# A transformer block on one core: seven products instead of eight in the down projection, and weight remainders on GpSimd

## The chip, the cores and the metric

The kernel runs on one core of one Trainium2 chip. TensorE multiplies matrices out of SBUF into PSUM (eight banks); VectorE, ScalarE and GpSimd work element by element, GpSimd on SBUF alone; SyncE only issues DMA transfers here. Each engine works off its own queue in order and waits on semaphores of the others. The time is microseconds (us) of the device for one execution.

## The reference

One pre-norm transformer block in float32, 2048 tokens of width 576: attention with 32 heads, then a gated feed-forward layer (GEGLU) with an inner width of 4608.

```python
h  = x + attention(layernorm(x), wqkv) @ wo
y  = layernorm(h)                             # 2048 x 576
g  = y @ w_gate                               # 576 x 4608
u  = y @ w_up                                 # 576 x 4608
h2 = h + (gelu(g) * u) @ w_down               # 4608 x 576
```

The change concerns the last three lines only, the feed-forward layer.

## The kernel before

**Two halves per number.** Every float32 operand of a matmul is scaled by a power of two and split into two float16 halves, `high = round(x)` and `low = x - high`. A product is then high·high + high·low + low·high, so three matmuls. Producing the two halves is work for ScalarE (the rounding, called `high` in the code) and VectorE or GpSimd (the remainder, called `low`).

**Tiling.** The inner width is cut into 18 chunks of 256 columns (`FC`); two chunks make a super chunk (`sc`, 0 to 8). The tokens are cut into two parts `p` of 1024, each of two blocks of 512 (`TB`).

**A unit** (`unit(c, p)`, line 1051) computes gate and up of one chunk for 1024 tokens, both by Strassen's scheme: seven products for gate and seven for up, alternating, each of 7 matmuls with 512 columns (`product`, line 1057). They go to six PSUM banks, g[0..2] and u[0..2]. Between products the other engines fetch the sums out of PSUM (`nc.scalar.copy`, `nc.vector.tensor_add`), apply `gelu` (ScalarE, L1070) and `gate` (VectorE, L1073), and split the result into float16 halves (`high`, ScalarE, L1076; `low`, GpSimd, L1079), the four pieces of `hts`. After each product the generator yields.

**A down stage** (`down(p, ...)`, line 1142) multiplies the pieces of two chunks with the super chunk's 512 rows of `w_down`: for each of 8 row blocks of 128 tokens and each half of the 576 columns one group of 12 matmuls with 288 columns, then one VectorE addition into the result `nat` (L1155).

**Weights.** `split_matrix` (line 927) prepares one chunk of `w_gate` or `w_up`: GpSimd forms the four sums that Strassen's scheme needs in place (L936), VectorE finds the largest magnitude (L129), a TensorE transpose spreads it (L138), VectorE turns it into a scale, ScalarE rounds three cuts of the seven pieces with that scale (L952) and VectorE subtracts (L966, L968). After the first cut's remainder the next matrix is loaded into the same place (`then`, L922 and L924). `split_down` (line 1021) does the like for `w_down`.

**Order.** Program order is kept on all engines (`manual_schedule`). The loop at line 1289 runs per super chunk: unit(c, 1), unit(c+1, 1), down(1), unit(c+2, 0), unit(c+3, 0), down(0), so the second half already works on the next super chunk. The preparation of weights is a second generator, `side`, and `beside` (line 1265) takes one step of it after each yield of a unit or a down stage, from yield number `head` on. Whatever such a step issues stands in each engine's queue right behind what the unit issued for the product just before.

Of the kernel before, what the change touches and what calls it, by code (L numbers as in the profile page):

```python
# [13 lines left out]
I32 = mybir.dt.int32  # L14
# [17 lines left out]
def tile_block(  # L32
# [61 lines left out]
    def view(region, off, shape, dtype=None):  # L94

        dtype = dtype or region.dtype
        v = region if dtype == region.dtype else region.bitcast(dtype)
        size = 4 if dtype == F32 else 2
        n = math.prod(shape)
        assert off % size == 0  # L100
        v = v[:, off // size : off // size + n]
        if len(shape) == 2:
            v = v.rearrange("p (a b) -> p a b", b=shape[1])
        elif len(shape) == 3:
            v = v.rearrange("p (a b c) -> p a b c", b=shape[1], c=shape[2])
        return v
# [61 lines left out]
    def pow2(e, a, b, name, pool=small):  # L168

        t = small.tile(list(e.shape), I32, tag=f"pi_{name}", name=f"pi_{name}")  # L170
        nc.vector.tensor_scalar(t, e, a, b, op0=ALU.mult, op1=ALU.add)
        r = pool.tile(list(e.shape), F32, tag=f"p_{name}", name=f"p_{name}")
        nc.vector.tensor_scalar(r.bitcast(I32), t, 23, None, op0=ALU.logical_shift_left)
        return r
# [127 lines left out]
    def run(it):  # L302
        for _ in it:
            pass
# [472 lines left out]

    VP = view(V, 0, (2 * PIECES, TB), F16)

    def piece(p, k):  # L780

        if k < 18:
            o = (2 * p + k // 9) * TB
            return XT[:, k % 9, o : o + TB]
        return VP[:, p * PIECES + k - 18]

    T4s = view(W, 23296, (HALF,), F32)

# [117 lines left out]
    dh = view(W, 6 * 2 * S, (4, D), F16)  # L906
    dl = view(W, 6 * 2 * S + 2 * 4 * D, (4, D), F16)
    hts = [[view(WK, 2 * 4 * TB * (2 * i + k), (4, TB), F16) for k in range(2)] for i in range(2)]
    ee = const.tile([P, 2, 2], I32, name="ee")

    def blank_rows():
# [15 lines left out]
    def split_matrix(c, m, hi_on=None, then=None, at=0, space=2, held=False):  # L927

        wh, wl = slots[c % 2][m]
        sums = [(nc.gpsimd.tensor_add, S1, A21, A22), (nc.gpsimd.tensor_sub, S2, S1, A11),  # L930
                (nc.gpsimd.tensor_sub, S3, A11, A21), (nc.gpsimd.tensor_sub, S4, A12, S2)]

        def add():
            if sums:
                op, d, a, b = sums.pop(0)
                op(W8[:, d], W8[:, a], W8[:, b])  # L936
# [15 lines left out]
        by = hi_on or (lambda dst, src, k: nc.scalar.activation(dst, src, AF.Copy, scale=k))  # L952
        cuts = ((4, 7), (0, 2), (2, 4))

        def high(k):
            if k < len(cuts):
                a, b = cuts[k]
                by(wh[:, a:b], W8[:, a:b], s)

        if held:  # L960
            yield "ready"
        high(0)
        yield
        for k, (a, b) in enumerate(cuts):
            high(k + 1)
            nc.vector.scalar_tensor_tensor(wl[:, a:b], W8[:, a:b, :2], s, wh[:, a:b, :2],  # L966
                                           op0=ALU.mult, op1=ALU.subtract)
            nc.vector.scalar_tensor_tensor(wh[r, a:b, 2], W8[r, a:b, 2], s[r], wh[r, a:b, 2],  # L968
                                           op0=ALU.mult, op1=ALU.subtract)
            if k == at and then is not None:  # L970
                then()
            yield
        if m == 0:
            scales[c % 2] = (pow2(e, 1, -20, f"gsc{c % 2}"), pow2(e, -1, 228, f"hsc{c % 2}"))

    scales = [None, None]

# [43 lines left out]
    def split_down(sc, at=(A, W8O)):  # L1021
# [22 lines left out]
        if at[0] is A:  # L1044
            blank_rows()

    banks = []
    tmps = []
    tmp_ring = ring(tmps)

    def unit(c, p):

        gsc, hsc = scales[c % 2]
        hh, hl = hts[c % 2]
        g, u = ([b[:, :TB] for b in banks[3 * i : 3 * i + 3]] for i in range(2))

        def product(m, bank, a, b, start):
            wh, wl = slots[c % 2][m]
            ks = [piece(p, 5 * b + k) for k in range(5)]
            mm = []  # L1060
            for k in range(2):
                mm += [(wh[:, a, k], ks[k]), (wh[:, a, k], ks[3 + k]), (wl[:, a, k], ks[k])]
            mm += [(wh[:, a, 2], ks[2])]
            for i, (w, x_) in enumerate(mm):
                nc.tensor.matmul(bank, w, x_, start=start and i == 0,  # L1065
                                 stop=i == len(mm) - 1,
                                 skip_group_check=not start)
# [10 lines left out]
        def low(i, j, v):  # L1078
            nc.gpsimd.tensor_sub(hl[:, 2 * i + j], v, hh[:, 2 * i + j])  # L1079

        xg, xu = next(tmp_ring), next(tmp_ring)
        product(0, g[0], A11, B11, True)
        nc.scalar.copy(xg, g[0])  # L1083
# [58 lines left out]
    def down(p, dsc, last):  # L1142
        for j in range(2):
            for i in range(TPB):
# [13 lines left out]
                if last:  # L1158
                    nc.sync.dma_start(ov[:, t], nat[:, t])


    def other_products():
        for b in range(1, NB):
# [125 lines left out]
    for sc in range(NCH // 2):  # L1289
        c = 2 * sc  # L1290
        last = sc == NCH // 2 - 1
        dsc = dscs[-1]
        if not last:
            g2, g3 = (split_matrix(c + 2, 0, None, lambda c=c: load_matrix(w_up, c + 2), held=True),
                      split_matrix(c + 3, 0, None, lambda c=c: load_matrix(w_up, c + 3)))
            u2, u3 = (split_matrix(c + 2, 1, None, lambda c=c: load_matrix(w_gate, c + 3)),
                      split_matrix(c + 3, 1, None, lambda sc=sc: load_down(sc + 1), 2))
            dn = split_down(sc + 1)
            side = chain(until_ready(g2))
        beside(unit(c, 1), side, head=0 if sc else 7)  # L1300
        run(side)
        if not last:
            side = chain(g2, pause(2), u2, pause(2), g3, pause(2), u3, pause(4), dn)
        beside(islice(u := unit(c + 1, 1), 13), side)
        run(u)
        beside(down(1, dsc, last), side, head=2)
        if last:
            break
        run(u2)
# [33 lines left out]
```

## Time and profile before

| what | value |
| --- | --- |
| runs | 2669.16, 2670.18, 2671.85 us, median 2670.18 |
| the profiled execution | 2668.08 us |
| its span, first to last instruction | 2666.3 us |
| TensorE matmuls busy over the span | 2589.7 us (97%) |
| VectorE, ScalarE, GpSimd busy | 2013.1, 1619.2, 777.3 us (76%, 61%, 29%) |
| granted TensorE clock, mean | 0.996 |

In the rows of the profile, PE is TensorE, PEld its weight loads, DVE is VectorE, ACT is ScalarE, POOL is GpSimd, SP is SyncE. A row of the timeline gives the start in the span, the duration, engine, source line, operation, output<-input, shape, count, and in brackets how long the engine sat idle before it and for whom. The feed-forward layer fills the span from about 1450 us on; the loop over super chunks repeats there every 132 us.

### The profile page before, as it was taken

To read this page: it belongs to the slowest core of one execution; us is meant where nothing else is said; L and a number is where in the kernel's file an instruction comes from. 1 tells how busy PE (TensorE), PEld (TensorE's weight loads), DVE (VectorE), ACT (ScalarE), POOL (GpSimd) and SP (SyncE) were. 2 spreads that over 40 slices of the span, in tenths; PEclk is the share of its full clock that TensorE was granted. 3 is DMA by queue.
4 is the path that set the end of the run, shared out by engine and by line. 5 is a ranking of instruction groups with operands and counts; after the bars stand their busy time and mean duration, and the time that the engine had idled before them with its cause. 6 is when DMAs were issued, how large, how long until landed. Compare 5 with 4: busy or idle time off the path is not lost.

```text
span 2666.3 us, 44517 instructions
## 1 busy us (share of the span) xinstructions
PE 2589.7 (97%) x16665; PEld 1118.6 (42%) x16665; DVE 2013.1 (76%) x3872; ACT 1619.2 (61%) x2128; POOL 777.3 (29%) x1040
## 2 busy tenths in 40 slices
PE   6999999999999999999999899999999999999999
PEld 2542222222222222222243555555555555555555
DVE  6367999999999999999967866566666666666653
ACT  5215999999999999999956433333333333333332
POOL 2200352132223232221666532222222222222221
PEclk9999999999999999999999999999999999999999
DMA  8411101010101010110116321010101010101010
GB/s 222 94 40 51 54 26 30 19 42 15 42 14 45 17 42 19 30 25 20 36 47 125 74 51 40 23 40 23 40 22 40 24 39 25 38 27 36 29 59 36
DMA packets 171466, 114.70 MB, mean 43 GB/s; under 512 B 90872, under 2 KB 149772, under 8 KB 171250
## 3 DMA queue, kind: packets, MB, share of 16 engines
q1 hardware_dynamic: 163566, 99.06, 13.9%
q0 software_dynamic: 7552, 12.79, 1.8%
q8 instruction: 130, 2.13, 0.3%
q14 instruction: 86, 0.70, 0.1%
q10 hardware_dynamic: 132, 0.01, 0.0%
HBM read 76.51 MB, written 15.01 MB: 34 GB/s over the span
## 4 chain that ended last, share of the span: by engine, by line
PE 67%; ACT 15%; issue 7%; DVE 4%; POOL 2%; DMA 2%; SPq 0%; ACTq 0%; DVEq 0%; POOLq 0%
PE more L1065 14%; PE bank L1065 13%; ACT WK L644 10%; PE bank L300 10%; PE bank L648 9%; PE more L300 8%; PE bank L589 7%; PE pair L300 4%; ACT nat L595 4%; PE pair L642 2%; DVE mx L601 1%; DMA nat<-rc 1%; ACT nat L662 0%; POOL A L996 0%; DMA V<-V 0%
## 5 line engine op out<-in xcount | busy, mean ns | idle before, releaser
L644 ACT ACTIVATE WK<-pair 128x1024 f32<-128x1024 f32 x1024 | 1000.0, 1041 | 84.8 <-PE pair L642 84.1
L601 DVE TENSOR_REDUCE mx<-bank 128x1 f32<-128x512 f32 x1552 | 975.7, 683 | 42.8 <-PE bank L589 32.4
L648 PE MATMUL bank<-WK,V 128*32 128x512 f32 x4096 | 547.7, 606 | 0.2 <-ACT nat L662 0.2
L300 PEld LDWEIGHTS <-WK 128*128 128x128 f16 x3456 | 338.0, 98 | 90.9 <-ACT WK L1076 1.7
L1065 PEld LDWEIGHTS <-W 128*128 128x128 f16 x2394 | 234.3, 98 | 282.9 <-issue 5.7
L589 PE MATMUL bank<-W 54*128 54x512 f16 x896 | 258.2, 379 | 14.0 <-DVE mx L601 1.8
L589 PE MATMUL bank<-A 54*128 54x512 f16 x904 | 255.0, 380 | 16.8 <-DVE mx L601 5.3
L671 POOL TENSOR_TENSOR rp<-rc,minus_one 128x16 f32<-128x16 f32 x28 | 81.9, 2926 | 537.1 <-DMA rc<-nat 537.1
L300 PE MATMUL more<-W,WK 128*128 128x288 f16 x1728 | 235.6, 286 | 2.2 <-ACT WK L1076 1.4
L300 PE MATMUL bank<-W,WK 128*128 128x288 f16 x1728 | 235.2, 286 | 0.0
L1065 PE MATMUL bank<-X,W 128*128 128x512 f16 x792 | 223.8, 379 | 0.0
L642 PE MATMUL pair<-A 56*128 56x512 f16 x1024 | 212.9, 381 | 2.3 <-ACT WK L644 1.4
L642 PE MATMUL pair<-W 56*128 56x512 f16 x1024 | 210.3, 380 | 4.3 <-ACT WK L644 3.2
L1065 PE MATMUL bank<-V,W 128*128 128x512 f16 x720 | 202.4, 379 | 0.4 <-ACT tmp L1115 0.3
L936 POOL TENSOR_TENSOR A<-A 128x384 f32<-128x384 f32 x136 | 137.0, 1028 | 202.6 <-DMA A<-in_B_w_up_dram 118.7
L589 PEld LDWEIGHTS <-W 54*128 54x128 f16 x1024 | 75.1, 93 | 283.6 <-issue 266.6
L599 DVE CUSTOM_DVE_ANT_0 nat<-bank,nat 128x512 f32<-128x512 f32 x248 | 171.4, 691 | 27.1 <-PE pair L642 4.4
L589 PEld LDWEIGHTS <-A 54*128 54x128 f16 x1024 | 72.3, 93 | 267.9 <-issue 250.8
L1079 POOL TENSOR_TENSOR WK<-tmp,WK 128x512 f16<-128x512 f32 x73 | 87.9, 1203 | 305.9 <-ACT WK L1076 305.6
L1083 ACT COPY tmp<-more 128x512 f32<-128x512 f32 x36 | 21.0, 583 | 236.8 <-PE more L1065 198.2
L595 ACT ACTIVATE nat<-bank 128x512 f32<-128x512 f32 x248 | 151.4, 611 | 11.5 <-PE bank L589 11.5
L648 PEld LDWEIGHTS bank<-WK,V 128*32 128x32 f32 x4096 | 81.1, 108 | 179.0 <-issue 164.2
(304 smaller groups left out, 3259.9 us busy)
## 6 DMA issues: line engine op xcount, KB each, us to landing
A<-in_B_w_down_dram SPq DMA_DIRECT2D x8, 1152.0 KB
nat<-rc SPq DMA_DIRECT2D x32, 256.0 KB
A<-in_B_w_gate_dram SPq DMA_DIRECT2D x64, 128.0 KB
A<-in_B_w_up_dram SPq DMA_DIRECT2D x64, 128.0 KB
qk_hi<-tmp SPq DMA_DIRECT2D x36, 128.0 KB
qk_lo<-tmp SPq DMA_DIRECT2D x36, 128.0 KB
out_dram<-nat SPq DMA_DIRECT2D x16, 288.0 KB
X<-nat SPq DMA_DIRECT2D x100, 36.0 KB
```

The source lines that it names most:

```text
L300: nc.tensor.matmul(dst, a, b, start=(i == 0), stop=(i == len(pairs) - 1))
L589: nc.tensor.matmul(pm[:, :TB], Q[r, q0 : q0 + P], keys, start=True, stop=True)
L595: nc.scalar.activation(row, pm[:, :TB], AF.Relu)
L599: nc.vector.tensor_tensor_reduce(row, pm[:, :TB], row, 1.0, LOWEST, ALU.add, ALU.max, dst)
L601: nc.vector.tensor_reduce(dst, pm[:, :TB], axis=AX.X, op=ALU.max)
L642: nc.tensor.matmul(pS[:, j, :TB], K[r, kt * P : (kt + 1) * P], Q[r, qc * TB : (qc + 1) * TB], start=True, stop=True)
L644: nc.scalar.activation(pes[(2 * kt + pr) % NPE], pS[:, :, :TB], AF.Exp, scale=ex_reg)
L648: nc.tensor.matmul(acc[32 * hh : 32 * hh + 32, :TB], Vg[n // NB][:, kt * G4 + hh * VC : kt * G4 + hh * VC + 32], pes[(2 * kt + hh // 2) % ...
L671: nc.gpsimd.tensor_tensor(rc, den, minus_one.to_broadcast([P, R]), op=ALU.pow)
L936: op(W8[:, d], W8[:, a], W8[:, b])
L1065: nc.tensor.matmul(bank, w, x_, start=start and i == 0, stop=i == len(mm) - 1, skip_group_check=not start)
L1079: nc.gpsimd.tensor_sub(hl[:, 2 * i + j], v, hh[:, 2 * i + j])
```

## The change

**Down by Strassen's scheme.** From super chunk 1 on the down stage is `down7`: seven products of 6 matmuls instead of eight blocks of 6, for each of four row blocks. It needs seven pieces of the gated activations instead of four (`unit7` forms H1 to H4 as sums and differences) and seven pieces of `w_down` (`split_down7`, sums on GpSimd). The unit's last products change places: A22 comes last, S4 before it. The PSUM banks change roles after each down stage.

**Remainders of gate and up weights.** From chunk 2 on ScalarE scales the float32 pieces in place and then rounds them, and GpSimd subtracts; the next load follows GpSimd's subtraction.

**Room.** The longer activation pieces lie where part of the layer's input pieces of tokens p=1 lay. The 15 input pieces that come last are stored to DRAM once for each p, and fetched in three parts, each after the product that used the old ones.

```diff
-    V = const.tile([P, 9936], F32, name="V")
+    V = const.tile([P, 10224], F32, name="V")
...
+    def keep_pieces(p):
+        nc.scalar.dma_start(xs[p], VP[:, p * PIECES + 2 : (p + 1) * PIECES])
+    def fetch_pieces(p, o):
+        nc.sync.dma_start(VP[:, 2 + 5 * o : 7 + 5 * o], xs[p][:, 5 * o : 5 * o + 5])
...
         def high(k):
             if k < len(cuts):
                 a, b = cuts[k]
-                by(wh[:, a:b], W8[:, a:b], s)
+                if c < 2:
+                    by(wh[:, a:b], W8[:, a:b], s)
+                else:
+                    nc.scalar.activation(W8[:, a:b], W8[:, a:b], AF.Copy, scale=s)
+                    nc.scalar.copy(wh[:, a:b], W8[:, a:b])
+        def low(a, b):
...
+            else:
+                nc.gpsimd.tensor_sub(wl[:, a:b], W8[:, a:b, :2], wh[:, a:b, :2])
+                nc.gpsimd.tensor_sub(wh[r, a:b, 2], W8[r, a:b, 2], wh[r, a:b, 2])
...
+    def split_down7(sc):
...
+        sums(0)
+        yield
+        high(0)
+        yield
+        low(0)
+        high(1)
+        sums(1)
+        yield
+        low(1)
+        high(2)
+        yield
+        low(2)
+        high(3)
+        yield
+        low(3)
+        yield
+        blank_rows()
...
+    def unit7(product, gelu, gate, g, u, hh, hl, used):
...
+        product(0, g[2], S4, B22, False)
+        nc.vector.tensor_add(ag, g[2], ag)
+        high(H22, bg)
+        gelu(ag, ag)
+        yield
+        product(1, u[2], S4, B22, False)
+        low(H22, bg)
+        nc.vector.tensor_add(au, u[2], au)
+        gate(ag, au)
+        nc.vector.tensor_add(xu, ag, bg)
+        yield
+        ga = next(tmp_ring)
+        product(0, g[0], A22, T4, False)
+        high(H1, xu)
+        gelu(ga, g[0])
+        low(H1, xu)
+        nc.vector.tensor_sub(bu, xu, xg)
+        high(H2, bu)
+        low(H2, bu)
+        yield
+        product(1, u[0], A22, T4, False)
+        used(2)
+        nc.vector.tensor_sub(au, xg, ag)
+        gate(ga, u[0])
+        high(H12, ga)
+        low(H12, ga)
+        high(H3, au)
+        low(H3, au)
+        nc.vector.tensor_sub(bg, ga, bu)
+        high(H4, bg)
+        low(H4, bg)
+        yield
...
+    def down7(p, dsc, last):
+        b0, b1, b2 = ((banks[i], banks[i + 3]) for i in (1, 0, 2))
+        def product(i, bank, a, b, start):
...
+            for k in range(2):
+                hh, hl = (v[:, a, tsl] for v in hts7[k])
+                mm += [(hh, dh7[:, k, b]), (hh, dl7[k][:, b]), (hl, dh7[:, k, b])]
...
+        for i0 in (0, 2):
+            for bank, a, b, start, outs in ((b0, H11, D11, True, ((0, 0),)),
+                                            (b2, H1, D1, True, ((1, 1),)),
+                                            (b0, H2, D2, False, ((0, 1),)),
+                                            (b1, H12, D21, True, ((0, 0),)),
+                                            (b0, H3, D3, False, ((1, 1),)),
+                                            (b2, H4, D22, False, ((0, 1),)),
+                                            (b0, H22, D4, False, ((1, 0),))):
+                for i in range(2):
+                    product(i0 + i, bank[i], a, b, start)
+                    add(i0 + i, bank[i], *outs)
+                yield
...
+            b0, b1 = b1, b0
+        banks[:] = [banks[i] for i in (1, 0, 2, 4, 3, 5)]
...
-            dn = split_down(sc + 1)
+            dn = split_down7(sc + 1)
...
-        beside(islice(u := unit(c + 1, 1), 13), side)
+        beside(islice(u := unit(c + 1, 1, None if last else lambda o: fetch_pieces(0, o)), 13), side)
         run(u)
-        beside(down(1, dsc, last), side, head=2)
+        beside(down7(1, dsc, last) if sc else down(1, dsc, last), side, head=2)
...
-        beside(unit(c + 3, 0), side)
+        beside(unit(c + 3, 0, lambda o: fetch_pieces(1, o)), side)
...
-        beside(down(0, dscs[-1], sc == NCH // 2 - 2), iter(()))
+        beside(down7(0, dscs[-1], sc == NCH // 2 - 2), iter(()))
```

More of the change, by code (lines that the diff above doesn't have):

```diff
@@ L778, in tile_block, with piece @@
     VP = view(V, 0, (2 * PIECES, TB), F16)
-    def piece(p, k):
+    xs = [dram.tile([P, 15, TB], F16, name=f"xs{i}") for i in range(2)]
+    def piece(p, k, c):
         if k < 18:
@@ L965, in split_matrix @@
             high(k + 1)
[L966 to L969, printed above, removed]
+            low(a, b)
             if k == at and then is not None:
@@ L1053, in unit @@
+    def unit(c, p, used=None):
         gsc, hsc = scales[c % 2]
         hh, hl = hts[c % 2]
+        hh7, hl7 = hts7[c % 2]
         g, u = ([b[:, :TB] for b in banks[3 * i : 3 * i + 3]] for i in range(2))
@@ L1058, in product @@
             wh, wl = slots[c % 2][m]
-            ks = [piece(p, 5 * b + k) for k in range(5)]
+            ks = [piece(p, 5 * b + k, c) for k in range(5)]
             mm = []
@@ L1079, in low @@
             nc.gpsimd.tensor_sub(hl[:, 2 * i + j], v, hh[:, 2 * i + j])
+        if c >= 2:
+            yield from unit7(product, gelu, gate, g, u, hh7, hl7, used or (lambda o: None))
+            return
         xg, xu = next(tmp_ring), next(tmp_ring)
```

119 lines of the change are left out of this document (115 added, 4 removed).

## The prediction

> **What bounds the kernel now.** I read the shares of the page first, then the busy time by stretches, then the timeline of each engine over one super chunk (1670 to 1802 us). The first row below is the page's head, the others are stretches: length, then busy time of TensorE, its weight loads, VectorE, ScalarE, GpSimd, then the granted clock.
>
> ```profile
> span 2666.3 us, 44517 instructions
> ...
> 1526.00:2662.00 1136.00, 1136.00 (x6741) 660.94 (x6739) 689.18 (x1339) 406.59 (x607) 297.05 (x276) 1.00 0.12 35
> ...
> 1670.04:1712.46 42.42, 42.42 (x200) 19.42 (x198) 23.86 (x47) 19.39 (x30) 12.30 (x11) 1.00 0.06 17
> 1712.46:1736.09 23.63, 23.63 (x195) 18.83 (x193) 17.36 (x34) 6.21 (x8) 5.07 (x5) 1.00 0.13 36
> ```
>
> From 1526 to 2662 us TensorE has no gap. In a pair of units (third row) VectorE is busy 23.86 of 42.42 us, ScalarE 19.39, GpSimd 12.30; in a down stage (fourth) VectorE 17.36 of 23.63. So TensorE alone sets the end here, and everything beside it has slack. The profiled execution took 2668.08 us, a span of 2666.3 and 1.8 around it; the median of the runs is 2670.18. I sum against 2668.08.
>
> ```profile
> 1711.05 1.67 PE L1065 MATMUL bank<-X,W 128*128 128x512 f16 x7
> 1712.56 1.63 PE L300 MATMUL more<-W,WK 128*128 128x288 f16 x12
> ...
> 1714.03 1.63 PE L300 MATMUL bank<-W,WK 128*128 128x288 f16 x12
> ```
>
> A product of 7 matmuls (512 columns) takes 1712.56 - 1711.05 = 1.51 us, a group of 12 (288 columns) 1714.03 - 1712.56 = 1.47, so 0.1225 each.
>
> **What the change saves.** A down stage had 16 groups of 12, 192 matmuls. Strassen's has 7 products for 4 row blocks of 6 matmuls, 168. It saves 24 x 0.1225 = 2.94 us, in 16 stages (both halves of eight super chunks): **47.0 us**. The units keep 98 matmuls each.
>
> **What it adds** lies on other engines. VectorE: 28 additions per down stage for 16, and 14 operations per unit for 10, less the low parts. ScalarE: 17 operations per unit for 14, and each weight piece twice (scale in place, then round). GpSimd: 7 low pieces per unit for 4, and the weights' low parts. In sums all of this fits. Whether it is in time is another matter: all four queues run in program order, and the change takes the slack out of the unit's end. I walk the queues there with these durations: a product's start, VectorE addition from PSUM, gating, ScalarE rounding, the operation behind it, GpSimd low piece, gelu.
>
> ```profile
> 1691.30 1.67 PE L1065 MATMUL more<-X,W 128*128 128x512 f16 x7
> ...
> 1691.50 0.69 DVE L1136 TENSOR_TENSOR W<-bank,W 128x512 f32<-128x512 f32 x1 [0.82 <-PE bank L1065]
> 1692.30 0.75 DVE L1073 SCALAR_TENSOR_TENSOR WK<-W,p_hsc,WK 128x512 f32<-128x512 f32 x1
> ...
> 1693.08 0.62 ACT L1076 CAST WK<-WK 128x512 f16<-128x512 f32 x1 [1.64 <-DVE WK L1073]
> 1693.61 0.58 ACT L1083 COPY tmp<-more 128x512 f32<-128x512 f32 x1
> ...
> 1693.78 1.16 POOL L1079 TENSOR_TENSOR WK<-WK 128x512 f16<-128x512 f32 x1 [2.59 <-ACT WK L1076]
> ...
> 1690.72 0.72 ACT L1070 ACTIVATE WK<-WK,p_gsc 128x512 f32<-128x512 f32 x1 [0.76 <-DVE WK L1132]
> ```
>
> An operation starts 0.20 us after the product it reads (1691.50, where the next product starts at 1691.30), 0.03 to 0.10 after another operation. An addition of two SBUF tiles isn't shown; its nearest rows are 0.69 and 0.75, I take 0.72 (either end moves nothing by over 0.2).
>
> **1. Unit into unit.** Until now the last two products write g[2] and u[2], and the next unit opens on g[0], free for two products. Now the last two (A22) write g[0] and u[0], and the next unit's first product waits for gelu(ga), which stands on ScalarE behind high(H1), which needs xu. From the end of the twelfth product: 0.20, addition 0.69, gating 0.75, xu 0.72, gaps 0.2, rounding 0.53, gelu 0.70: 3.85, against 3.02 for the two products. TensorE waits **0.83** even with nothing beside it. At least 0.5, with crowding 1.6. In the first half (tokens p=1) of super chunks 1 to 8: 8 x 0.83 = 6.6.
>
> **2. Unit into down, p=1.** The side work of the second unit, by its steps (one per product): at the twelfth VectorE forms the scale of the next up matrix and ScalarE cuts its first piece, at the thirteenth the second piece and the first low part. These are the same steps as now:
>
> ```profile
> 1710.48 0.28 DVE L142 TENSOR_REDUCE ab_m<-bank 128x1 f32<-128x128 f32 x1
> ...
> 1711.42 0.15 DVE L173 TENSOR_SCALAR p_s_m<-pi_s_m 128x1 int32<-128x1 int32 x1
> ...
> 1711.61 1.25 ACT L952 ACTIVATE W<-A,p_s_m 128x1152 f16<-128x1152 f32 x1 [0.39 <-DVE p_s_m L173]
> ...
> 1713.38 0.92 ACT L952 ACTIVATE W<-A,p_s_m 128x768 f16<-128x768 f32 x1
> 1716.17 0.62 ACT L1076 CAST WK<-WK 128x512 f16<-128x512 f32 x1 [1.86 <-DVE WK L1073]
> ...
> 1716.86 1.16 POOL L1079 TENSOR_TENSOR WK<-WK 128x512 f16<-128x512 f32 x1 [4.41 <-ACT WK L1076]
> ...
> L999 POOL TENSOR_TENSOR WK<-A,W x4: 671/1157/1161, 1366.1 to 1390.8; 128x512 f16<-128x512 f32 x3, 128x256 f16<-128x256 f32 x1
> ...
> L1000 POOL TENSOR_TENSOR W<-A,W x4: 422/664/666, 1367.4 to 1392.0; 32x256 f16<-32x256 f32 x3, 32x128 f16<-32x128 f32 x1
> ```
>
> Now the last ScalarE rounding (1716.17) and GpSimd piece (to 1718.02) come 5.5 us after the down stage's start at 1712.56 and nobody waits: they are read in its second half, 8 x 1.47 = 11.8 us in. After the change H1 is read in the second step. From the twelfth product's end: 3.6 us to the scale (2.5 as above to xu, 1.1 from 1710.48 to the scale), first piece twice 2 x 1.20 = 2.4 on ScalarE (in place isn't shown; 1.25 is the same size into f16, I take it), H1's rounding 0.6, low piece 1.2: 7.8, and 0.9 more because VectorE arrives late at the twelfth step (3, below). TensorE needs it 3.02 + 1.47 + 0.61 = 5.1 in: 3.7 us of waiting. Then H12's low piece stands on GpSimd behind the up matrix's first low part (768 columns by 1.157 and 0.671: 1.64, and 0.91 on 32 partitions, 2.55), which costs 1.8 more. **5.5** (2.9 with VectorE in time and GpSimd free), in super chunks 1 to 7, which have side work: 38.5. The other pieces then arrive 0.3 to 0.7 us ahead.
>
> **3. Later loads.** A matrix is loaded once the first low part of the matrix before has left its place.
>
> ```profile
> 1695.37 1.02 DVE L966 SCALAR_TENSOR_TENSOR A<-A,p_s_m 128x768 f16<-128x768 f32 x1 [2.33 <-ACT A L952]
> ...
> 1696.46 0.38 SPq L922 DMA_DIRECT2D A<-in_B_w_up_dram  x1
> ...
> 1704.78 0.95 DVE L129 TENSOR_REDUCE ac_m<-A 128x1 f32<-128x768 f32 x1 [1.54 <-DMA A<-in_B_w_up_dram]
> ...
> 1704.71 4.00 POOL L936 TENSOR_TENSOR A<-A 128x384 f32<-128x384 f32 x4 [2.06 <-DMA A<-in_B_w_up_dram]
> ...
> 1707.92 0.27 PE L138 MATMUL bank<-id,am_m 128*128 128x128 f32 x1
> ```
>
> Now it goes 0.07 us from the end of VectorE's low part (1695.37 + 1.02), and the second half is there 8.3 us after the first issue. VectorE waits 1.54 us at 1704.78; the maximum's transpose stands after the eleventh product, at 1707.92, 2.0 us after the maximum's parts are there, and TensorE doesn't wait. After the change ScalarE does 2.4 for 1.25 and GpSimd 2.55 for 1.02, behind the unit's own pieces: the load goes 3.7 us later. VectorE gets the maximum at 18.4 us from the unit's nominal start, TensorE asks at 17.4: **1.1** x 7 = 7.7. The same with the second up matrix (p=0): its load goes after a GpSimd low part, **1.25** x 7 = 8.8. Bounds: 0 and 2.5 each.
>
> **4. Units with p=0.** A down stage gives 12 side steps for 14, so each later side step falls two products later. The second up matrix is now cut in products 9 to 11 of the unit. Behind its scale (2.0 after product 9, and 0.6 for GpSimd's last sum, which must have read the pieces before ScalarE scales them) ScalarE has 2.4 + 0.6 + 1.75 + 0.55 + 0.6 + 1.75 + 0.55 + 0.7 = 8.9 us up to gelu(ga): 11.5, less 0.1 of overlap, against 5 x 1.51 = 7.55. **3.8** (bounds 0.83 and 4.5) x 7, and 0.8 in super chunk 0, whose down stage is the old one: 27.4.
>
> **5. Down weights.**
>
> ```profile
> 1755.35 0.38 SPq L1016 DMA_DIRECT2D A<-in_B_w_down_dram  x1
> ...
> 1762.23 2.61 DVE L129 TENSOR_REDUCE ac_dn<-A 128x1 f32<-128x1152 f32 x2 [3.03 <-DMA A<-in_B_w_down_dram]
> ...
> 1775.73 0.81 DVE L1041 SCALAR_TENSOR_TENSOR W<-A,p_s_dn,W 128x576 f16<-128x576 f32 x1
> ...
> 1780.67 0.52 DVE L1155 SCALAR_TENSOR_TENSOR nat<-more,p_dsc,nat 128x288 f32<-128x288 f32 x1
> ...
> 1779.00 1.63 PE L300 MATMUL more<-W,WK 128*128 128x288 f16 x12
> ```
>
> The load lands 6.9 us after issue and VectorE already waits 3.03. The last low part ends at 1776.54, 2.5 us before the down stage starts at 1779.00. Now it comes two steps later by the count of 4 and one more by its own (product 13 for 10): 4.5 us, behind six VectorE operations of 5.4 us from the twelfth product on where 3.5 remain to the first use (1.9), with VectorE 1.2 late there already. **3.1** (0.5 to 4) x 7 = 21.7. Its load waits for GpSimd's last low part, so its maximum is late at the transpose by **1.5** (0 to 2.5) x 7 = 10.5.
>
> **Costed at nothing.** VectorE's 28 additions in a down stage: 28 x 0.52 = 14.6 of 20.6 us with some 5 us of side work; a bank has 2.2 us until it is written again; uncovered, 0.5 a stage. The pieces' stores and fetches (0.66 MB each beside a 1.2 MB load of 6.9 us) are used 20 us later; uncovered, 4 us each. The end gets a few output tiles at once: 1.0.
>
> **Sum.** 6.6 + 38.5 + 7.7 + 8.8 + 27.4 + 21.7 + 10.5 + 1.0 = 122.2 lost, 47.0 won: 2668.1 + 75.2 = **2743**.
>
> That such waits do hold TensorE is shown where units first ran with other work in the queues:
>
> ```profile
> 1508.69 1.67 PE L1065 MATMUL more<-X,W 128*128 128x512 f16 x7 [1.64 <-DVE W L1112]
> ...
> 1514.32 0.42 PE L300 MATMUL more<-W,WK 128*128 128x288 f16 x2 [1.35 <-ACT WK L1076]
> 1515.56 0.30 PE L300 MATMUL more<-W,WK 128*128 128x288 f16 x1 [0.82 <-POOL WK L1079]
> ```
>
> There it waited in turn for a VectorE addition, a ScalarE rounding and a GpSimd piece.
>
> **Rivals.** *The queues catch up (faster).* Each wait of TensorE lets the others draw level; if the side work of one super chunk then finds its place, only 0.83 at 15 boundaries is left: 2668.1 - 47.0 + 12.5 + 1.0 = 2635. The low shares speak for it, the fixed program order against. It turns at 47.0 / 8 = 5.9 us of waiting per super chunk; I count 17. Chance 0.16. *Half of it:* loads and down weights stay hidden (terms 3 and 5 at nothing), 2668.1 - 47.0 + 6.6 + 38.5 + 27.4 + 1.0 = 2695. Chance 0.18. *Balance* within 0.2% (5 us, about what can be told from no change): 0.06. *The clock drops:*
>
> ```profile
> 20.41 7.71 PE L300 MATMUL bank<-X,W 128*128 128x512 f16 x35 [3.08 <-DMA X<-A]
> ...
> 76.45 3.95 PE L300 MATMUL pair<-W,X 128*128 128x288 f16 x19 [4.32 <-ACT V L368]
> ...
> 20.40:24.00 3.60, 3.59 (x17) 1.67 (x18) 0.00 (x0) 0.37 (x1) 0.00 (x0) 1.00 0.96 297
> 76.40:80.00 3.60, 3.55 (x19) 2.40 (x19) 0.68 (x1) 0.78 (x4) 2.22 (x4) 0.62 0.45 85
> ```
>
> After a gap of 3.08 us TensorE went on at clock 1.00, after 4.32 at 0.62 for 3.6 us. If my waits of 3.8 and 3.1 count as long ones, each costs 0.38 x 3.6 = 1.4: 14 x 1.4 = 20, 2763. Chance 0.15. The Trainium skill, TensorE: Matmul & The Clock Gate, Why this matters for your kernels, bars gaps over some 3 us, as one idle window halves the clock; by that rule all these waits pay, and the 3.08 us row doesn't agree. *Contention:*
>
> ```profile
> L1073 DVE SCALAR_TENSOR_TENSOR A<-tmp,p_hsc,A x34: 750/751/1551, 1554.7 to 2634.2; 128x512 f32<-128x512 f32 x34
> ```
>
> The gating of two SBUF tiles takes 751 ns at the median and up to 1551. Seven such operations per unit for three, three of them in term 1's chain, would add up to 0.8 a link, 16 x 1.6 = 26 us at most: in the range, not in the sum. The Trainium skill, GPSIMD Engine Reference, Key points, has GpSimd share its SBUF interfaces with VectorE operations of two SBUF inputs; that speaks against this change, and the spread of the row agrees.
>
> **Numbers.** My forecast (2715 to 2760) has 0.45. Slower 0.45 + 0.18 + 0.15 = 0.78, same 0.06, faster 0.16. The range, 2650 to 2785, leaves out most of the faster case and the worst of clock and contention together.
>
> **To be seen after.** Some 47 us less TensorE busy time in matmuls; gaps of about 0.8 us ahead of every second unit of p=1; ahead of H1's matmuls in the p=1 down stage a wait for ScalarE's rounding and GpSimd's piece; ahead of the second unit of p=0 one for ScalarE; ahead of the p=0 down stage one for VectorE's low part; GpSimd busy share in the stage from 26% (297 of 1136 us) to over 50%. I am wrong if TensorE stays at full busy in the stage, or if it waits for fetches.

## The result and the profile after

The changed kernel took 2822.57 us (median of 4 runs, 2820.86 to 2823.98), the kernel before beside it 2671.01 (2669.16 to 2672.09): a ratio of 1.0568, 95% interval 1.055 to 1.0586. The direction is as forecast; the size, 152 us, is outside the range, whose upper end was 2785.

The head of the changed kernel's page, and below it the feed-forward stage in the view by windows (length; busy time and count of TensorE, its weight loads, VectorE, ScalarE, GpSimd; granted clock; DMA share; GB/s):

```profile
span 2822.2 us, 44927 instructions
...
PE 2607.1 (92%) x16281; PEld 1096.2 (39%) x16281; DVE 2138.4 (76%) x4000; ACT 1766.2 (63%) x2320; POOL 1181.5 (42%) x1392
```

```profile
1526.00:2818.00 1292.00, 1156.34 (x6386) 640.91 (x6383) 817.47 (x1473) 555.56 (x802) 704.06 (x630) 0.95 0.19 57
```

Before, TensorE was busy through all of the feed-forward stage at a clock of 1.00. Now it is idle for 1292.00 - 1156.34 = 136 us of it, and the clock that it was granted is 0.95 on average. No other engine is anywhere near full: VectorE 63%, GpSimd 54%, ScalarE 43% of the stretch. By these shares the engines have room on average; what they lack is to be in time at certain places.

TensorE's waits in that stage, by what ended them (total us, times, longest; rows below 2 us are left out):

```profile
PE more L1235 <- ACT tmp L1240: 38.3, 16, 4.3
PE more L1346 <- DVE V L1111: 28.9, 8, 3.8
PE more L1346 <- ACT V L1141: 22.9, 8, 3.1
PE more L1346 <- ACT W L1107: 18.5, 7, 2.9
PE bank L138 <- DVE am_m L133: 8.7, 8, 2.2
PE more L1346 <- POOL V L1144: 7.6, 10, 1.3
PE more L138 <- DVE am_m L133: 6.7, 7, 1.4
```

L1235 is a unit's matmul, L1346 one of the new down stage, L138 the transpose of a maximum. They wait for gelu (L1240), for a low or high part of the down weights (L1111, L1107), for a rounding or a GpSimd piece of the activations (L1141, L1144), for the parts of a maximum (L133). One super chunk in the timeline of TensorE has the longest of them; it lasts 2242.15 - 2089.30 = 152.85 us, where it was 132 before:

```profile
2089.30 3.14 PE L1235 MATMUL more<-X,W 128*128 128x512 f16 x7 [4.27 <-ACT tmp L1240]
...
2116.15 0.28 PE L1346 MATMUL more<-W,V 128*128 128x288 f16 x1 [2.49 <-ACT W L1107]
...
2120.23 0.40 PE L1346 MATMUL more<-V 128*128 128x288 f16 x1 [3.80 <-DVE V L1111]
...
2164.66 1.67 PE L1235 MATMUL more<-X,W 128*128 128x512 f16 x7 [0.58 <-ACT tmp L1240]
...
2192.70 0.30 PE L1346 MATMUL more<-W,V 128*128 128x288 f16 x1 [3.15 <-ACT V L1141]
2193.93 0.42 PE L1346 MATMUL more<-W,V 128*128 128x288 f16 x1 [0.81 <-POOL V L1144]
...
2242.15 3.15 PE L1235 MATMUL more<-X,W 128*128 128x512 f16 x7 [4.21 <-ACT tmp L1240]
```

The first and last row also show the clock: seven matmuls take 3.14 us instead of 1.67. Three windows around the first one:

```profile
2084.10:2087.50 3.40, 0.93 (x5) 0.29 (x3) 3.17 (x5) 3.29 (x5) 3.20 (x3) 1.00 0.00 0
2087.60:2094.30 6.70, 5.00 (x12) 1.72 (x12) 5.70 (x5) 3.79 (x7) 6.54 (x5) 0.50 0.19 42
2094.40:2097.80 3.40, 3.40 (x17) 1.52 (x16) 1.24 (x2) 1.27 (x3) 3.40 (x4) 1.00 0.64 251
```

TensorE works 0.93 us of the first window; the granted clock is then at half for about 6.8 us and comes back. The trace has 22 such spells between 1530 us and the last matmul, 133 us in all; TensorE was busy in 106 of them, so some 53 us of its time went there.

Why the queues are late is read on ScalarE in the same place, the last products of a unit with p=0:

```profile
2079.67 1.26 ACT L973 ACTIVATE A<-A,p_s_m 128x1152 f32<-128x1152 f32 x1 [4.05 <-POOL A L948]
2080.96 1.15 ACT L974 CAST W<-A 128x1152 f16<-128x1152 f32 x1
2082.02 0.72 ACT L1240 ACTIVATE A<-A,p_gsc 128x512 f32<-128x512 f32 x1
2082.64 0.92 ACT L973 ACTIVATE A<-A,p_s_m 128x768 f32<-128x768 f32 x1
2083.59 0.83 ACT L974 CAST W<-A 128x768 f16<-128x768 f32 x1
...
2088.57 0.68 ACT L1240 ACTIVATE tmp<-more,p_gsc 128x512 f32<-128x512 f32 x1
```

ScalarE first stood idle 4.05 us for a sum on GpSimd (L948), then scaled in place and rounded (L973, L974), and the gelu that the next unit's first product waits for came at 2088.57. Each of these cuts takes ScalarE nearly twice as long as before (1.26 + 1.15 for 1.25, 0.92 + 0.83 for 0.92).

### The profile page after: what moved, and what is told of

The parts are those of the page before. It is cut to its first block, busy times and chain, and to the rows that moved or that the text cites. A ratio compares the mean times of both kernels' runs of the same rounds, so it can differ in the third digit from the quotient of the medians.

```text
span 2822.2 us, 44927 instructions
## 1 busy us (share of the span) xinstructions
PE 2607.1 (92%) x16281; PEld 1096.2 (39%) x16281; DVE 2138.4 (76%) x4000; ACT 1766.2 (63%) x2320; POOL 1181.5 (42%) x1392
## 4 chain that ended last, share of the span: by engine, by line
PE 41%; ACT 21%; issue 11%; DVE 11%; DMA 6%; POOL 6%; SPq 3%; ACTq 0%; POOLq 0%; DVEq 0%
ACT WK L644 10%; PE bank L648 8%; PE bank L589 6%; PE more L1235 6%; PE bank L1235 5%; ACT nat L595 4%; PE bank L1346 4%; PE more L1346 4%; PE pair L300 3%; PE bank L300 3%; DMA A<-in_B_w_up_dram 2%; PE pair L642 2%; ACT A L973 2%; POOL A L948 1%; SPq L936 1%
## 5 line engine op out<-in xcount | busy, mean ns | idle before, releaser
L1235 PEld LDWEIGHTS <-W 128*128 128x128 f16 x2394 | 238.8, 100 | 337.3 <-issue 72.8
L1235 PE MATMUL bank<-X,W 128*128 128x512 f16 x792 | 232.3, 392 | 0.0
L973 ACT ACTIVATE A<-A,p_s_m 128x768 f32<-128x768 f32 (+1 forms) x96 | 99.7, 1038 | 172.3 <-DVE p_s_m L173 148.2
L1235 PE MATMUL bank<-V,W 128*128 128x512 f16 x720 | 202.4, 379 | 0.4 <-ACT tmp L1288 0.3
L1346 PEld LDWEIGHTS <-V 128*128 128x128 f16 x1344 | 137.4, 103 | 127.3 <-issue 50.2
L1346 PE MATMUL more<-W,V 128*128 128x288 f16 x448 | 127.7, 302 | 49.0 <-ACT V L1141 22.9
L1235 PE MATMUL more<-X,W 128*128 128x512 f16 x468 | 128.9, 405 | 41.0 <-ACT tmp L1240 38.3
L948 POOL TENSOR_TENSOR A<-A 128x384 f32<-128x384 f32 x136 | 137.8, 1031 | 63.0 <-DMA A<-in_B_w_up_dram 49.0
L1346 PEld LDWEIGHTS <-WK 128*128 128x128 f16 x1344 | 138.6, 103 | 48.4 <-issue 3.7
```

Of the source, the lines that this page charges most:

```text
L973: nc.scalar.activation(W8[:, a:b], W8[:, a:b], AF.Copy, scale=s)
L1235: nc.tensor.matmul(bank, w, x_, start=start and i == 0, stop=i == len(mm) - 1, skip_group_check=not start)
L1346: nc.tensor.matmul(bank[:, :HALF], w, x_, start=start and n == 0, stop=n == len(mm) - 1, skip_group_check=not start)
```

## The experiments

Each kernel is one execution beside one of the kernel before on the same chip (2671.68 to 2672.92). Executions of the changed kernel lie within 3.2 us of each other, so differences over some 5 us are read as real, smaller ones are not.

**e1_vector_low: the weights' pieces as before** (one ScalarE pass, low parts on VectorE), the rest as changed.

```diff
-                if c < 2:
+                if True:
                     by(wh[:, a:b], W8[:, a:b], s)
...
-            if c < 2:
+            if True:
                 nc.vector.scalar_tensor_tensor(...)
```

> Strassen's down stage kept; the weights' pieces as in the kernel before (ScalarE rounds once with the scale, VectorE forms the remainder). Theory Q (time is lost in waits at the unit's end, because the weight pieces stand ahead of the unit's own pieces in the queues, and in the half clock after these waits): the load goes some 3.7 us earlier again, ScalarE's burst is 2.8 us shorter; the wait ahead of the second unit of p=0 falls from 4.2 to about 1 us, the one for H1 from 3.9 to about 1.6, the transposes wait no more; 2670 to 2710 us. Theory S (Strassen's down itself costs: additions on VectorE, sums kept in PSUM, fetches): stays above 2780.

2810.29 us: only 12 less. Q falls; the time is in the range of S, against which e4 below speaks. The waits for late maxima are gone (15.4 us in the changed kernel) and the one for H1's rounding is 12.5 us instead of 22.9, but the one for gelu, which was to shrink to about 1 us, stays (40.1 us in 16 places, the longest 4.8), and there is a new one:

```profile
PE more L1346 <- DVE nat L1353: 20.5, 8, 2.8
```

VectorE's additions out of the down stage's banks (L1353) are now late; in the changed kernel this row has 1.6 us. That the low parts now hold up VectorE's queue instead of GpSimd's is the likely reason, which this run alone does not show.

**e2_pieces_only: the kernel before with GpSimd's low parts and the scaling in place alone**, no Strassen down. 

> The kernel before with the weights' pieces of the change alone (scaled in place by ScalarE, remainder on GpSimd, from chunk 2 on), the eight-product down stage and the old unit kept. Theory Q: the old unit has some 5 us of slack at its end, so only the later loads tell, in waits of 1 to 2 us for the transposes: 2670 to 2700 us. Theory C (GpSimd and VectorE get in each other's way, ScalarE's double work costs by itself): above 2740.

```diff
+                    nc.scalar.activation(W8[:, a:b], W8[:, a:b], AF.Copy, scale=s)
+                    nc.scalar.copy(wh[:, a:b], W8[:, a:b])
...
+                nc.gpsimd.tensor_sub(wl[:, a:b], W8[:, a:b, :2], wh[:, a:b, :2])
```

2700.13 us, at the upper edge of Q, 27 slower than before (2672.86), clock 0.995. TensorE waits most for two copies out of PSUM on ScalarE, 13.2 us in 8 places and 4.4 in 9, and for late maxima, 7.4 in 11. So this half of the change costs 27 us in the old order of work.

**e3_fill_waits: useless matmuls in the three long waits**, so that the clock stays up.

```diff
+    def busy(n):
+        for _ in range(n):
+            nc.tensor.matmul(singles[3][:, :TB], id16, XT[:, 0, :TB], start=True, stop=True)
```

12 in front of H1's matmuls, 17 before the second unit of p=0, 9 and 15 in the second down stage.

> The changed kernel with products of no use put on TensorE into its three long waits per super chunk (12 ahead of H1's second half, 17 ahead of the second unit of p=0, 9 and 15 ahead of the p=0 down stage's first use of the late down weights), each shorter in sum than the wait it fills. Theory Q with the clock as a part of its own: the ends of the waits stay where they are, the clock stays at 1.00, and 55 to 67 us go: 2755 to 2770 us. If the waits alone make the loss and the low clock is only beside them: within 10 us of 2822.

2810.84 us, again 12 less: far from the first case, just outside the second. The stage by windows, and TensorE's timeline in a super chunk:

```profile
1526.00:2804.00 1278.00, 1204.62 (x6815) 665.79 (x6812) 819.13 (x1474) 555.68 (x804) 706.37 (x631) 1.00 0.19 57
```

```profile
2085.28 1.67 PE L1235 MATMUL more<-X,W 128*128 128x512 f16 x7 [0.62 <-ACT tmp L1240]
2087.83 1.67 PE L1235 MATMUL bank<-X,W 128*128 128x512 f16 x7 [0.88 <-DVE tmp L1243]
...
2119.29 0.53 PE L1352 MATMUL more<-W,WK 128*128 128x288 f16 x3 [0.84 <-DVE nat L1359]
```

The clock is 1.00 and the filled places still have a rest of 0.5 to 0.9 us on average, so the filling itself held nothing up: 17 matmuls of 0.216 us and the rest of 0.62 make 4.29 us, as long as the wait of 4.27 before. But behind them stand waits that were not there (0.88 for the gating, 0.84 for an addition). By the list of waits those for additions, gating, GpSimd's pieces and the down weights' maxima come to 33.6 us, 9.2 in the changed kernel. So it reads as if the other engines caught up while TensorE ran at half clock; at full clock it waits for them instead. With the queues as they are, a full clock is worth about 12 us.

**e4_no_side: no preparation of weights from super chunk 1 on** (stale weights are used).

```diff
-        if not last:
+        if sc == 0:
             side = chain(g2, pause(2), u2, pause(2), g3, pause(2), u3, pause(4), dn)
```

> The changed kernel without the preparation of gate, up and down weights from super chunk 1 on (neither loads nor pieces; the units go on with the weights that lie there). Theory Q: nothing stands in the queues beside the unit, only the 0.58 us into every second unit are left: 2668 - 47 + 16 x 0.58 = 2630, between 2622 and 2645 us, clock 1.00. Theory S: above 2700.

2648.92 us, 24 less than before (2672.86), 4 above what was expected. In the later super chunks only unit into unit waits, 0.58 at both halves, and a super chunk takes 2218.74 - 2091.49 = 127.25 us:

```profile
2091.49 1.67 PE L1235 MATMUL more<-X,W 128*128 128x512 f16 x7 [0.58 <-ACT tmp L1240]
...
2218.74 1.67 PE L1235 MATMUL more<-X,W 128*128 128x512 f16 x7 [0.58 <-ACT tmp L1240]
```

The units' new end and Strassen's down stage fit by themselves. The loss comes with the preparation of weights that runs beside them.

**e6_two_steps_later: 11 instead of 13 side steps in the second unit of p=1, the two moved into the down stage**, away from H1.

```diff
-lambda o: fetch_pieces(0, o)), 13), side)
+lambda o: fetch_pieces(0, o)), 13 if sc == 0 or last else 11), side)
...
-side, head=2)
+side, head=0 if sc else 2)
```

> The changed kernel with the side work's steps 12 and 13 (scale and first cuts of the next up matrix) moved from the second unit's last products to the first two steps of the p=1 down stage, in super chunks 1 to 7; nothing else is moved. Both theories: the waits for H1's rounding and GpSimd piece (3.1 and 0.8 us per super chunk) go. Theory Q (each wait is a loss of its own): 7 x 3.9 us and the slow clock behind that wait go too, 2770 to 2790 us. Theory P (the preparation of the weights - load, maximum, scale, pieces, next load - is one chain that sets the pace, and TensorE waits for it now here, now there): the same time comes back as longer waits in the down stage and ahead of the second unit of p=0, 2805 to 2830 us.

2814.26 us, as P has it. H1's wait for ScalarE is down to 1.3 us, the one for its GpSimd piece stays against what both theories had (9.1 us, 7.6 in the changed kernel), and now VectorE's additions are late, 20.8 us in 12 places: they stand behind a maximum whose load isn't there yet.

**e7_no_loads: gate and up weights, and the next down weights, are not loaded again** (all the rest of the preparation runs, on stale data).

```diff
-            g2, g3 = (split_matrix(c + 2, 0, None, lambda c=c: load_matrix(w_up, c + 2), held=True),
+            g2, g3 = (split_matrix(c + 2, 0, None, lambda: None, held=True),
```

> The changed kernel without the loads of gate, up and down weights from chunk 2's up matrix on (the pieces are cut over and over from what lies there); all work of the engines is kept. Theory P: the loads' some 8 us each, three or four of them in the chain of a super chunk, are gone, and the time falls by over 60 us, below 2760, with the waits ahead of the second unit of p=0 and of the p=0 down stage mostly gone. Theory Q: only the transposes' waits (1.4 and 0.6 us) and what VectorE loses waiting for loads go, 2790 to 2810 us.

2782.87 us, between the two: the loads are worth 40 us. The waits for gelu (35.4) and down weights (28.8 and 17.5) stay.

**e8_head0: two more side steps in each down stage of p=1**, 14 as before, none taken from the units.

```diff
-side, head=2)
+side, head=0 if sc else 2)
```

> Two more steps of the side work in each down stage of tokens p=1 (14 as in the kernel before, for 12), none taken from the units. If the late weights of the second down stage are a loss of their own (some 6 us per super chunk after the change), that loss goes: 2775 to 2785 us. If the preparation of the weights sets the pace as a whole and TensorE only waits for it in one place or another: 2810 to 2834, with the waits moved.

2809.99 us, at the lower edge of the second case (the waits have moved). The wait for down weights goes from 47.4 (28.9 and 18.5) to 18.3, but the waits for the rounding and the GpSimd pieces of the activations go from 30.5 to 45.6:

```profile
PE more L1346 <- ACT V L1141: 30.1, 15, 3.1
...
PE more L1346 <- POOL V L1144: 15.5, 18, 1.3
```

**e9_one_pass, e10_tiny_lows, e11_both: the pieces of gate and up weights made cheaper**, by their parts: no scaling in place, low parts on 16 columns only, and both.

```diff
-                    nc.scalar.activation(W8[:, a:b], W8[:, a:b], AF.Copy, scale=s)
...
-                nc.gpsimd.tensor_sub(wl[:, a:b], W8[:, a:b, :2], wh[:, a:b, :2])
+                nc.gpsimd.tensor_sub(wl[:, a, 0, :16], W8[:, a, 0, :16], wh[:, a, 0, :16])
```

> Leaves out the scaling in place of gate and up weights from chunk 2 on, so ScalarE passes over each piece once and rounds the unscaled one. If the chain of preparation sets the pace, the pass counts once per matrix and more in the queue, 5 to 8 us per super chunk: 2765 to 2790 us. If only the local waits count (H1 behind the first piece twice): 2805 to 2815.

> Leaves out the low parts of gate and up weights from chunk 2 on but for 16 columns, so GpSimd gives out the next load some 2.5 us sooner per matrix and runs less beside VectorE. If the chain of preparation sets the pace: 2740 to 2765 us. If only local waits count: 2795 to 2805.

> Leaves out both, the scaling in place and all but 16 columns of the low parts. If the pieces of the weights are what takes the gain: 2690 to 2720 us. If the order of the queues at the units' end costs it whatever the pieces take: 2780 to 2795.

2768.89, 2793.98 and 2732.67 us: the second ScalarE pass is worth 54, the low parts on GpSimd 29, both together 90, close to their sum (82). e9 fits the chain of preparation, e10 comes out 1 us below the case of local waits, e11 lies between its two cases, nearer the first. With both gone, e11 has these waits left:

```profile
PE more L1345 <- DVE V L1110: 28.6, 8, 3.8
PE more L1345 <- ACT W L1106: 17.4, 7, 2.5
PE more L1345 <- DVE nat L1352: 16.6, 7, 2.4
PE more L1234 <- ACT tmp L1239: 9.4, 16, 0.6
```

The gelu's wait has shrunk to 0.6 at each unit, as without any preparation. The two rows of the down weights have hardly moved: the first has 28.8 in e1, e7 and e9, 28.9 in e10, 28.6 here, the second 17.4 to 17.8 in all five, 18.5 in the changed kernel. Something else sets these waits.

**e12_both_head0 and e13_both_no_dn: e11 with two more side steps in the down stage, and that without the next down weights** (neither loaded nor cut).

```diff
-side, head=2)
+side, head=0 if sc else 2)
...
-            dn = split_down7(sc + 1)
+            dn = iter(()) if sc else split_down7(sc + 1)
```

> Leaves out the scaling in place and all but 16 columns of the low parts, as the run before, and gives each down stage of tokens p=1 two more side steps (14). With the queues this light, two steps sooner should help the late down weights (6.3 us per super chunk without it): if waits are losses of their own once the queues have room, 2695 to 2712 us; if they only move, 2722 to 2738.

> Leaves out the scaling in place, all but 16 columns of the low parts, and from super chunk 1 on the load and the pieces of the next down weights. If the late down weights are 6.3 us per super chunk and the half clock behind them: 2665 to 2685 us, with VectorE's additions behind blocked maxima (2.4 per super chunk) left. If another side step takes their place: above 2700.

2705.54 and 2670.16 us, both within what was expected if waits are losses of their own once the queues have room. Of e11's time 2732.67 - 2670.16 = 62.5 us are gone: 27.1 by the two side steps, 35.4 more without the load and the pieces of the down weights. VectorE's timeline of the changed kernel, in the last products before the second down stage:

```profile
2110.45 1.64 DVE L1111 SCALAR_TENSOR_TENSOR W<-A,p_s_dn,W 128x1152 f16<-128x1152 f32 x1
2112.01 0.68 DVE L1194 TENSOR_TENSOR WK<-bank,WK 128x512 f32<-128x512 f32 x1
2112.80 1.37 DVE L1243 SCALAR_TENSOR_TENSOR WK<-WK,p_hsc 128x512 f32<-128x512 f32 x1
2114.20 1.17 DVE L1196 TENSOR_TENSOR V<-WK,A 128x512 f32<-128x512 f32 x1
2115.29 2.00 DVE L1111 SCALAR_TENSOR_TENSOR V<-A,p_s_dn,W 128x864 f16<-128x864 f32 x1
2117.21 1.64 DVE L1203 TENSOR_TENSOR tmp<-V,tmp 128x512 f32<-128x512 f32 x1
2118.77 1.41 DVE L1111 SCALAR_TENSOR_TENSOR V<-A,p_s_dn,W 128x1152 f16<-128x1152 f32 x1
```

There is hardly a gap from 2110.45 to 2120.18. The low part of the down weights that TensorE waits for (2118.77 + 1.41, TensorE goes on at 2120.23) stands behind two other low parts and four operations of the unit. Four such low parts of 864 and 1152 columns take the place of four of 576 (0.81 us each before).

There is a second chain, on GpSimd and ScalarE:

```profile
2110.08 0.80 POOL L1096 TENSOR_TENSOR A<-A 128x288 f32<-128x288 f32 x1 [4.96 <-DVE W L1111]
...
2113.65 1.01 ACT L1107 ACTIVATE W<-A,p_s_dn 128x864 f16<-128x864 f32 x1 [2.35 <-POOL A L1098]
```

GpSimd writes its sums for the second chunk of the down weights (L1096 to L1099) to the place from which VectorE takes the first chunk's low part, so it stands idle until that low part is done (36.2 us in 8 places). ScalarE in turn stands idle for these sums (19.9 us in 8 places) before it rounds the second chunk, and TensorE waits for the rounding (18.5 us). The pieces of gate and up weights have no part in this chain, which fits that the two rows hardly moved without them. No run gave the sums a place of their own, so what this link costs by itself is not shown.

**e14_five_of_six: TensorE's work taken away instead**: one of the six matmuls of each down product is left out.

```diff
                 mm += [(hh, dh7[:, k, b]), (hh, dl7[k][:, b]), (hl, dh7[:, k, b])]
+            del mm[1]
```

> The changed kernel without one of the six matmuls of each down product from super chunk 1 on (the one with the down weights' low part of the first chunk), so TensorE has 28 x 0.1225 = 3.4 us less to do in each of 16 down stages, 55 us in all, and nothing else is changed but that the other queues get less time per product. If TensorE's work, its waits and its slow spells add up as in the prediction's sum: 2760 to 2775 us. If the other engines' chain sets the pace of the super chunk and TensorE waits for it in one place or another: 2808 to 2826, with as much more waiting.

2784.33 us: 38 of the 55 us come back, so neither theory holds alone. The waits stay as they are (gelu 38.2, L1111 29.0), and so does most of the rest: TensorE is idle for 140 us of the stage (135 before) and the spells at half clock last 157 us (133 before), 23 of 6.8 us. So work taken off TensorE inside the down stages saves time for the most part, and the waits around the units' ends do not grow to fill it.

## Why the prediction was right in direction and wrong in size

**The waits came where they were forecast, but for the down weights.** By the prediction's own terms, from the waits after (the row for gelu split by 0.58 at 8 places for term 1, the rest for term 4):

| term | forecast | measured |
| --- | --- | --- |
| 1. unit into unit, p=1 | 6.6 | 8 x 0.58 = 4.6 |
| 2. H1 and H12 in the p=1 down stage | 38.5 | 22.9 + 7.6 = 30.5 |
| 3. transposes of late maxima | 7.7 + 8.8 = 16.5 | 8.7 + 6.7 = 15.4 |
| 4. gelu into the second unit of p=0 | 27.4 | 38.3 - 4.6 = 33.7 |
| 5. low part of the down weights | 21.7 | 28.9 |
| 5. transposes of the down weights' maxima | 10.5 | no row |
| rounding of the down weights, in no term | 0 | 18.5 |
| sum | 121.2 | 131.6 |

Terms 1 to 4 come to 84.2 us for 89.0. In term 5 the transposes did not wait, and a wait that the prediction does not have, for ScalarE's rounding behind GpSimd's sums, took 18.5 us. (Some addends do not give the figure stated: those of term 1 make 3.79 us, not 3.85, and 8.7 - 5.1 in term 2 is 3.6, not 3.7; nothing hangs on it.) The fetches of stored pieces, put at nothing, have no row either.

**Strassen's saving held.** In a super chunk without preparation (e4) the kernel takes 127.25 us; before it took 2331.72 - 2199.42 = 132.30. So 5.05 of the nominal 5.88 us arrive, with two waits of 0.58 added and the preparation's transposes missing on TensorE.

**The step that failed is what the sum takes for granted behind each wait**: that everything is level again, TensorE at full clock and the pieces "0.3 to 0.7 us ahead". Spans went from 2666.3 to 2822.2, and with the 47.0 saved that is 202.9 us lost where 122.2 were forecast. The waits of the table make 131.6 of it. Some 53 us are TensorE's work at half clock: 22 spells, 133 us, of which it was busy in 106. The prediction kept the clock as a rival of its own with 20 us (14 spells of 3.6 us) and a chance of 0.15, and put nothing for it into the sum. A smaller part is starting again: a wait is counted from the end of a product of 1.67 us, but products in a row follow each other by 1.51, so each of the stage's 73 waits costs some 0.16 more, an estimate of 12 us in all.

The Trainium skill, TensorE: Matmul & The Clock Gate, Why this matters for your kernels, bars gaps over some 3 us; the trace of this stage agrees, where every wait of 2.99 us and more was followed by half clock. The forecast set a single row of 3.08 us without a fall against it, and that row was luck: at the same place, some 20 us from the start, a wait of 2.53 us was followed by a clock of 0.56 in e12 (20.4 to 24.0 us) and one of 2.98 by 0.65 in e8, while 3.28 in e7 and 2.99 in the changed kernel left it at 1.00.

**But the clock is not what has to be mended.** e3 held it at 1.00, as the sum had assumed, and the time was 2810.84, not 2743. Some 24 us of new waits stood behind the filled ones. The forecast walked each queue with undisturbed durations and let all engines be level behind each wait; they weren't. By experiments the loss comes apart so:

| what | forecast | measured |
| --- | --- | --- |
| Strassen's down stage and the units' new end alone (e4 against before) | -47.0 + 6.6 + 1.0 = -39 | -24 |
| preparation without the added pieces and without down weights (e4 to e13) | 0 | +21 |
| down weights (e13 to e11) | +32 | +62.5 |
| second ScalarE pass and low parts on GpSimd (e11 to changed) | 16.5 + 27.4 + 38.5 = +82 | +90 |
| sum | +75 | +150 |

Measured are single steps in this one order, e13 with two more side steps; in another order the parts would differ (the two steps won 12.6 us in e8 and 27.1 in e12). So the fourth row was right. **Term 5 was mis-sized by 30 us**: VectorE's longer low parts and the chain over GpSimd's sums. The preparation beside the new unit, put at nothing, costs 21, mainly VectorE's additions behind a full queue at the down stage's start (17.4 us in e13's waits), for which the prediction had "uncovered, 0.5 a stage". Most of the first row's 15 us are waits that remain: 0.58 also at p=0, where only p=1 was counted, and those of the first super chunks, where e4 still prepares weights (gelu 12.9 us in all, once 3.8; others 6.2).

**The rivals.** Queues did not catch up, nor did half of it stay hidden: loads and down weights, which that rival has at nothing, were worth 40 us (e7) and 62.5 (e11 to e13). Contention was left out of the sum as at most 26 us. In the groups by line of the changed kernel from 1800 to 2700 us (behind the bar busy us, mean ns of one, idle time before):

```profile
L1203 DVE TENSOR_TENSOR tmp<-V,tmp 128x512 f32<-128x512 f32 x24 | 27.2, 1134 | 0.4
L1243 DVE SCALAR_TENSOR_TENSOR WK<-WK,p_hsc 128x512 f32<-128x512 f32 x24 | 26.5, 1105 | 3.6 <-ACT WK L1240 2.3
L1215 DVE TENSOR_TENSOR A<-tmp 128x512 f32<-128x512 f32 x23 | 25.0, 1087 | 2.4
```

The same lines of e4, where GpSimd has only the units' pieces to do, from 1800 to 2560 us:

```profile
L1203 DVE TENSOR_TENSOR tmp<-V,tmp 128x512 f32<-128x512 f32 x24 | 16.6, 692 | 0.8
L1243 DVE SCALAR_TENSOR_TENSOR WK<-WK,p_hsc 128x512 f32<-128x512 f32 x24 | 18.0, 751 | 2.8 <-DVE WK L1194 0.5
L1215 DVE TENSOR_TENSOR A<-tmp 128x512 f32<-128x512 f32 x24 | 18.4, 767 | 2.5
```

An operation on two SBUF tiles took 0.32 to 0.44 us longer, in just the links that the forecast priced at 0.72. The Trainium skill, GPSIMD Engine Reference, Key points, says that GpSimd shares its SBUF interfaces with VectorE operations of two SBUF inputs; the trace agrees. Of the 60 operations of L1196, L1203 and L1209 between 1800 and 2560 us in the changed kernel, the 25 with no GpSimd subtraction beside them took 0.68 to 0.69 us, the 20 with one for nine tenths of their time or more 1.04 to 1.64. The loads are not the reason (L1203 takes 1.16 us on average in e7), and the weights' low parts are not the only one: with these on VectorE again (e1) it takes 1.14. Contention and clock were each given as alternatives to the forecast; both came in addition to it, and the range had no room for that.

**What stays open.** How much of the 90 us of the pieces is contention and how much queueing was not separated. Of the 17 us of removed TensorE work that did not come back in e14, some 12 are found as more waiting and more half clock (5 and 7 us); why these grew is not shown. No kernel tried beat the one before with all its work done.

## What to carry to other kernels

A product saved on TensorE is worth something only if the other engines' queues can still deliver at the same borders: before making TensorE shorter, check the borders where all side work is in program order, not the busy shares, which here stayed at 43 to 63%. Walking the queues with undisturbed durations found most of the waits here, but what follows a late queue came on top: add clock and contention to the sum instead of holding them as rivals, and follow each place that is written again to the last engine that reads it. To find what to mend, fill the waits with useless work and take the side work away piece by piece: the first showed that the clock was for the most part a symptom, the second put prices on the parts.

## What the runs showed of the hardware

Spells at half clock come in whole steps: those after 1530 us in the changed kernel are 3.4 or 6.8 us long (two of 10.2 in e11), and each began within 5 us of the start of a wait. A wait of about 2.4 us may bring one or not. In e11 the same place, matmuls behind 2.37 or 2.38 us of waiting, comes seven times, and one of them brought a spell:

```profile
2149.32 0.53 PE L1345 MATMUL more<-W,WK 128*128 128x288 f16 x3 [2.38 <-DVE nat L1352]
...
2008.02 0.53 PE L1345 MATMUL more<-W,WK 128*128 128x288 f16 x3 [2.37 <-DVE nat L1352]
```

```profile
2150.10:2153.30 3.20, 3.20 (x16) 1.94 (x14) 1.41 (x5) 0.13 (x1) 3.04 (x6) 0.50 0.49 140
...
2008.30:2011.60 3.30, 3.30 (x30) 2.63 (x28) 2.85 (x7) 0.62 (x1) 3.24 (x4) 1.00 0.36 104
```

The first was followed by half clock, the second by full clock, so the length of a gap alone does not decide it. The one that fell had another wait of 0.73 us just ahead; but so had one that did not, at 1725.69 us (0.67, then 2.37). In the changed kernel's stage the clock fell behind every single wait of 2.99 us and more and behind every pair of 2.5 to 2.9 and 3.8, and not behind single ones of 2.16 and 2.29.
